# The last stage of a gradient kernel: a row-wise side for its products, left rows turned on TensorE, input rows in mid-column

## The chip, the cores and the metric

The kernel runs on one core of one Trainium2 chip. The metric is device time in microseconds (us) of one execution. The engines: TensorE (PE, matmuls; PEld loads its weights), VectorE (DVE), ScalarE (ACT), GpSimd (POOL) and SyncE (SP). SP, ACT and POOL also issue DMAs, each on a queue of its own and in the order of its program; the profile calls POOL's queue q0, SP's q1 and ACT's q10.

## The reference, cut to what matters

A layer normalisation feeds two branches whose outputs are added to the input: an attention with a recurrent memory (64 segments of 32 rows, 8 memory rows handed from segment to segment, 32 heads of 128) and a dense layer with squared relu. The kernel computes the output and all gradients for a given `grad_out`.

```python
for s in range(n_seg):
    h = jnp.concatenate([mem, xs], axis=1)          # 8 memory rows and 32 rows of the segment
    q, k, v = (jnp.einsum('btd,dhe->bhte', h, W) for W in (Wq, Wk, Wv))
    scores = jnp.where(mask, jnp.einsum('bhqe,bhke->bhqk', q, k) * scale, -1e9)
    o = jnp.einsum('bhqk,bhke->bhqe', softmax(scores), v)
    o = jnp.einsum('bhte,hed->btd', o, Wo)
    mem = o[:, :M, :]
    outs.append(o[:, M:, :])
...
return x + A(xn) + B(xn)
_out, _vjp = jax.vjp(f, A_x, A_mem0, A_Wq, A_Wk, A_Wv, A_Wo, B_w1, B_b1, B_w2, B_b2)
_grads = _vjp(grad_out)
```

What matters here are the gradients of the four attention weights. Each is one large product over all 2560 rows (2048 rows of segments and 64 times 8 memory rows): for Wq, Wk and Wv the normalised rows, transposed, times the gradient of q, k or v; for Wo the attention's rows, transposed, times the gradient of the output rows. The gradient of the input rows needs one more pass over 16 blocks of 128 rows.

## The kernel before, in words

The work is done in five stages: the dense branch, the forward chain over 64 segments, a preparation of the memory rows, the backward chain over the segments from last to first, and the last stage. Four segments make a block of 128 rows; there are NB = 16 blocks. Each block has also 32 "left" rows, the memory rows of its four segments.

**The backward chain** (lines 1088 to 1392). `B_ORDER` is a list, written out by hand, of the operations of one block's four steps, and `play` (line 581) walks it. A name with `L.` in front is an operation of a block's left rows; `+` and `-` shift it to the next or the one before. Each engine runs its instructions in this order. What the change touches:

- `gl` (line 1198) loads GT, a block's gradient rows with the feature axis on the partitions ([128, 4, 128]), on SP. The steps overwrite GT's memory rows by the gradients handed back (`HTf`).
- `gs` (line 1148) stores GT into the DRAM tensor S_GM on SP, in that same layout. The load of the GT after next waits for this store, since GT has two buffers.
- `vtr` (line 1245) is a DMA transpose of v on SP into b_vl; POOL copies it to b_vT (line 1252), and TensorE's scores and products follow.
- `so` (line 1151) stores the gradients of q, k and v into S_GB. `nt` and its store (lines 1184 to 1191) transpose a block's left rows gvL, gkL and gqL by DMA to gNat and store them into S_GL. For the last block (b = 0) both are issued by ACT instead of SP.
- `xt` (line 1177) reduces the left rows' input gradients to b_XL on VectorE (line 476), in one buffer, and `sl` (line 1181) stores it into S_XGL on SP.
- At the end the first memory's gradient is transposed by TensorE (line 1389), copied out of PSUM by VectorE to gm (line 1391) and stored. gm takes the memory of the buffer gON, which the last block's gNat of v uses as well.

**The last stage** (lines 1397 to 1508) goes over 16 "columns" (`COLS`: which weight, which quarter of its 4096 columns). A column's data is one tile gn of [128, 20, 1024] (16 blocks, then 4 tiles of left rows), in three buffers taken in turn: p5a lies over Wo and the chain's gv, p5b and p5c over the other weights. `rows_of` (line 1414) fills it: the Wo columns by plain loads of S_ON and S_OL, the others by 16 DMA transposes of S_GB on SP and plain loads of S_GL. Columns 0 and 1 are loaded on POOL's queue, later ones on SP's. Column i + 2 is loaded as column i starts.

The other side of the product is resident: GOc [128, 20, 512] for the Wo columns and HNc for the rest. `slot_side` (line 1406) fills each by four DMA transposes on SP (of S_GM, of S_HT) and four plain loads of left rows.

Per column TensorE makes eight products into eight PSUM banks, each a sum of 20 matmuls (line 1505): in column 0 the eight go side by side, block by block in `ORDER` (15 down to 0, then the left ones); in the others one product after the other. `leave` (line 1474) copies each out of PSUM on ScalarE and stores it on POOL's queue. Behind each column `input_rows` (line 1442) handles one block of input rows: five loads on POOL's queue (XT, XL, gb, xn, gi), a copy on VectorE (line 1448), four transposes on TensorE into ps_rows (line 1457), some arithmetic on VectorE, ScalarE and POOL, and a store. The loads at the stage's beginning are issued in the program's order (`manual_schedule`); the order of the rest is left to the scheduler.

Of the kernel before, what the change touches and what calls it, by code (L numbers as in the profile page):

```python
# [10 lines left out]
BF16 = mybir.dt.bfloat16  # L11
# [15 lines left out]
def kernel(  # L27
# [93 lines left out]
    S_GM = dram.tile([P, DC, S], BF16, name="S_GM")  # L121
# [815 lines left out]
    with sb("la", 2) as la, sb("ls", 2) as ls, sb("lo", 1) as lo_, sb("wg", 2) as wg, psum("lpp", 1) as lpp, psum("lr", 4) as lr:  # L937
# [168 lines left out]
    with sb("bq", 1) as bq, sb("bt", 1) as bt, sb("bs", 2) as bs, sb("be", 1) as be, psum("bpp", 1) as bpp, psum("br", 4) as br:  # L1106
# [17 lines left out]
        def block(b):  # L1124
            if b not in blk:
# [3 lines left out]
                          "XT": (bt, [P, DC, SPB, SEG], F32), "R4": (bt, [P, D], F32)}  # L1129
# [7 lines left out]
        def left(b):  # L1137
# [10 lines left out]
            o["gs"] = lambda: dma(S_GM[:, :, b * P:(b + 1) * P], gts[b][:])  # L1148
# [34 lines left out]
            for t, n in enumerate("qkv"):  # L1183
                def nt(n=n):

                    tag = "gNat" if b > 0 else {"k": "gNat", "v": "gON", "q": "gOT"}[n]
                    st[n] = bt.tile([P, KH, P], BF16, name="gNat", tag=tag)
                    (nc.sync if b > 0 else nc.scalar).dma_start_transpose(st[n][:], B_[src[n]][:].rearrange("p k g r -> p k (g r)"))
                o[n + "tr"] = nt
                o[n + "st"] = lambda n=n, t=t: (dma if b > 0 else nc.scalar.dma_start)(S_GL[b].rearrange("g r t c -> (g r) t c")[:, t, :],  # L1190
# [207 lines left out]
    with sb("p5a", 1) as p5a, sb("p5h", 1) as p5h, sb("p5", 2) as p5, sb("p5g", 1) as p5g, \  # L1398
            sb("p5b", 1, "right") as p5b, sb("p5c", 1, "right") as p5c, \
            tc.tile_pool(name="p5ps", bufs=8, space=bass.MemoryType.PSUM) as p5ps:  # L1400
# [5 lines left out]
        def slot_side(t_, srcT, src):  # L1406
            for dc in range(DC):
                nc.sync.dma_start_transpose(t_[:, 0:NB, dc * P:(dc + 1) * P], srcT[:, dc, :])
            lv = src.rearrange("(c q r) d -> c q r d", q=16, r=SEG)
            for c in range(NLC):  # L1410
                dma(t_[:, NB + c, :], lv[c][:, 0:M, :])
            return t_

        def rows_of(i, g, blocks, left_):

            t_ = (p5a, p5b, p5c)[i % 3].tile([P, RC_ALL, CW], BF16, name="gn5", tag="gn%d" % (i % 3))
            q = pdma if i < 2 else dma
            if blocks is None:
                for b in range(NB - 4, -1, -4):
                    q(t_[:, b:b + 4, :], S_ON[b:b + 4, g].rearrange("b p c -> p b c"))  # L1420
            else:
                for b in range(NB - 1, -1, -1):
                    nc.sync.dma_start_transpose(t_[:, b, :].rearrange("p (k e) -> p k e", k=KH),
                                                blocks(b)[:, g].rearrange("p k r -> p (k r)"))
            for j in range(SPB):
                q(t_[32 * j:32 * j + 32, NB:RC_ALL, :], left_(g).rearrange("(c j) r x -> j r c x", j=SPB)[j])
            return t_


        COLS = [(3, 0), (3, 1), (2, 0), (2, 1), (2, 2), (3, 2), (2, 3), (1, 0), (1, 1), (1, 2), (3, 3), (1, 3), (0, 0),  # L1430
                (0, 1), (0, 2), (0, 3)]
        got = {}

        def loads(i):
            if i < len(COLS):
                t, g = COLS[i]
                if t == 3:
                    got[i] = rows_of(i, g, None, lambda g: S_OL[:, g])
                else:
                    got[i] = rows_of(i, g, lambda b: S_GB[b, t], lambda g: S_GL[:, g, :, t, :])  # L1440

        def input_rows(b):

            XT = p5.tile([P, DC, P], F32, name="XT5", tag="XT5")
            pdma(XT[:], S_XG[b])
            XL = p5.tile([P, DC, SPB, M], F32, name="XL5", tag="XL5")
            pdma(XL[:], S_XGL[b])
# [96 lines left out]
```

## Time and profile before

| what | value |
|---|---|
| time of three runs (median) | 3051.87, 3058.38, 3061.96 us (3058.38) |
| the profiled execution, from first to last instruction | 3059.8 us; no other time of it is listed |
| PE, PEld, DVE, ACT, POOL busy | 88%, 45%, 43%, 33%, 22% |
| DMA | 566.78 MB, mean 185 GB/s; q1 58.8% of the 16 engines' span, q0 13.5%, q10 0.4% |
| mean granted clock of TensorE | 0.971 |
| matmuls of the last stage (line 1505) | 2560, 379 to 385 ns each in the mean, overlapping |
| copies out of PSUM in the last stage (line 1476) | 128, 586 ns |

How to read it: an instruction's row has its start and its length in us, its engine, line, operation and tiles (out<-in), and in brackets how long the engine sat idle before it and what ended that. "SPq" or "ACTq" is a queue's sequencer: the time there is the issue of a DMA, not its transfer. The chain of waits follows the work that ended last back through what released each step. A share of DMA of 1.00 means that all 16 engines are busy.

### The profile page before, as it was taken

How to read it: one execution, taken by the hardware profiler on the slowest of the kernel's cores; microseconds unless marked ns; L12 is line 12 of the kernel's file. 1: busy time of each engine (PE TensorE's matmuls, PEld its weight loads, DVE VectorE, ACT ScalarE, POOL GpSimd, SP SyncE). 2: the span in 40 equal slices, each digit the busy share in tenths (PEclk: the TensorE clock that was granted, in tenths of full speed). 3: DMA queues.
4: the chain of work that ended last, by engine and by line, in shares of the span. 5: the costliest groups of instructions: out<-in, count | busy, mean ns of one | idle time of the engine just before them, and what ended most of it. 6: DMA issues, size and time to landing. Idle time of an engine off the chain costs nothing. (4 is left out here: it accounts for less than half of the span.)

```text
span 3059.8 us, 109712 instructions
## 1 busy us (share of the span) xinstructions
PE 2705.4 (88%) x48600; PEld 1386.8 (45%) x48600; DVE 1319.5 (43%) x3581; ACT 994.7 (33%) x2306; POOL 658.0 (22%) x1264
## 2 busy tenths in 40 slices
PE   8997899999999886877799899998989559999998
PEld 4453444444444444446444444444444224444443
DVE  5452566666666664334345444544545201100010
ACT  2422444444444444323333333333333101111111
POOL 0000000000000000113343433434343213322222
PEclk9998999999999998999999999999999879999999
DMA  9548375766767767777577676776777899898991
GB/s 257 185 146 250 101 188 161 189 181 172 190 168 182 165 157 192 229 230 220 149 173 174 190 187 164 177 203 169 176 200 175 238 192 217 194 211 207 204 207 39
DMA packets 794559, 566.78 MB, mean 185 GB/s; under 512 B 579409, under 2 KB 681570, under 8 KB 790754
## 3 DMA queue, kind: packets, MB, share of 16 engines
q1 hardware_dynamic: 748322, 430.47, 58.8%
q0 software_dynamic: 40528, 126.53, 13.5%
q8 instruction: 381, 6.24, 0.9%
q10 hardware_dynamic: 5232, 2.75, 0.4%
q14 instruction: 96, 0.79, 0.1%
HBM read 193.61 MB, written 238.56 MB: 141 GB/s over the span
## 5 line engine op out<-in xcount | busy, mean ns | idle before, releaser
L1505 PE MATMUL ps_gw<-gn,HNc 128*128 128x512 bf16 x1920 | 416.4, 379 | 0.0
L1505 PEld LDWEIGHTS <-HNc 128*128 128x128 bf16 x1920 | 187.8, 98 | 223.9
L374 ACT CAST f_N<-ps_proj 128x512 bf16<-128x512 f32 x320 | 185.9, 581 | 243.9 <-PE ps_proj L392 223.4
L1476 ACT CAST wt<-ps_gw 128x512 bf16<-128x512 f32 x128 | 74.4, 586 | 503.5 <-PE ps_gw L1505 474.4
L392 PEld LDWEIGHTS <-X 128*32 128x32 bf16 x6144 | 153.3, 97 | 161.3 <-DVE X L482 13.9
L835 POOL COPY kM<-f_kT 128x256 bf16<-128x256 bf16 x64 | 25.6, 401 | 786.7 <-DVE f_kT L377 594.9
L1459 DVE TENSOR_TENSOR gx<-ps_rows,gb 128x512 f32<-128x512 f32 x16 | 11.1, 692 | 420.5 <-PE ps_rows L1457 418.2
L1505 PE MATMUL ps_gw<-GOc,gn 128*128 128x512 bf16 x640 | 142.2, 385 | 54.8 <-DMA GOc<-S_GM 54.8
L460 PE MATMUL ps_gR<-Wk,gk 128*32 128x512 bf16 x2048 | 146.7, 386 | 19.4 <-ACT gk L374 12.9
L392 PE MATMUL ps_proj<-Wk,X 128*32 128x512 bf16 x2048 | 135.4, 384 | 12.6 <-DVE X L482 6.9
L460 PE MATMUL ps_gR<-Wq,gq 128*32 128x512 bf16 x2048 | 141.6, 382 | 1.2 <-issue 1.2
L374 ACT CAST gk<-b_pp 128x256 bf16<-128x256 f32 x192 | 68.8, 377 | 208.3 <-PE b_pp L547 146.6
L1477 POOL DMA_DIRECT2D out_dram<-wt x128 | 69.2, 541 | 309.5 <-ACT wt L1476 309.4
L1239 POOL COPY PD<-b_P 32x320 bf16<-32x320 bf16 x256 | 114.9, 449 | 95.3 <-PE b_pp L1292 64.4
L460 PE MATMUL ps_gR<-Wv,gv 128*32 128x512 bf16 x2048 | 133.4, 379 | 0.3 <-issue 0.3
L392 PE MATMUL ps_proj<-Wo,GT 128*32 128x512 bf16 x2048 | 123.9, 384 | 7.9 <-POOL GT L1203 6.7
L392 PE MATMUL ps_proj<-Wq,X 128*32 128x512 bf16 x2048 | 128.7, 382 | 0.0
L460 PE MATMUL ps_R<-Wo,OT 128*32 128x512 bf16 x2048 | 126.4, 388 | 0.0
L469 PE MATMUL ps_sum<-identF,R 128*128 128x128 f32 x512 | 102.4, 295 | 24.6 <-ACT R L374 18.4
L392 PE MATMUL ps_proj<-Wv,X 128*32 128x512 bf16 x2048 | 124.1, 378 | 0.0
L1505 PEld LDWEIGHTS <-gn 128*128 128x128 bf16 x640 | 63.4, 99 | 132.3 <-issue 59.6
L374 ACT CAST gON<-ps_proj 128x512 bf16<-128x512 f32 x128 | 74.9, 585 | 143.2 <-PE ps_proj L392 141.5
(260 smaller groups left out, 5128.0 us busy)
## 6 DMA issues: line engine op xcount, KB each, us to landing
S_A<-f_N SPq DMA_DIRECT2D x64, 512.0 KB
out_dram<-wt POOLq DMA_DIRECT2D x142, 128.0 KB, 4.6
S_A<-f_N SPq DMA_DIRECT2D x64, 256.0 KB
S_GB<-gv SPq DMA_DIRECT2D x32, 512.0 KB
S_GB<-gq SPq DMA_DIRECT2D x32, 512.0 KB
S_GB<-gk SPq DMA_DIRECT2D x32, 512.0 KB
b_kN<-S_A POOLq DMA_DIRECT2D x63, 256.0 KB, 5.0
b_qN<-S_A POOLq DMA_DIRECT2D x63, 256.0 KB, 5.4
```

The costliest lines, as they stand in the source:

```text
L374: nc.scalar.copy(out, in_)
L392: nc.tensor.matmul(o, lhsT=hT[:, dc, :], rhs=x, start=(dc == 0), stop=(dc == DC - 1), tile_position=(0, 32 * g))
L460: nc.tensor.matmul(o, lhsT=XT(k, g), rhs=x, start=(first and k == 4 * h), stop=(last and k == 4 * h + 3), tile_position=(0, 32 * g))
L469: nc.tensor.transpose(st["T"][:, c * P:(c + 1) * P], R4()[:, c * P:(c + 1) * P], identF[:])
L835: o["km"] = lambda: nc.gpsimd.tensor_copy(B_["kM"][:, :, :, lc], T["kT"][:, :, :, 0:M])
L1239: nc.gpsimd.tensor_copy(PD[32 * g:32 * g + 32, g], C["P"][32 * g:32 * g + 32, :, 0:L])
L1459: nc.vector.tensor_tensor(out=gx[:], in0=ps[:], in1=gb[:], op=ALU.add)
L1476: nc.scalar.copy(wt[:], ps[:])
L1477: pdma(dst, wt[:])
L1505: nc.tensor.matmul(ps[:], lhsT=l(rc), rhs=r(rc), start=(n == 0), stop=(n == RC_ALL - 1))
```

## The change

- S_GM takes the gradient rows row-wise, [16, 128, 512]. In the chain `gs` turns GT by a DMA transpose on SP into a new tile GN (one buffer), and a new operation `gst` stores GN into S_GM. For the last block TensorE turns GT in four transposes, and ScalarE copies the result out.
- `nt` turns the last block's left rows on TensorE, in two halves of four transposes for each of v, k and q, copied out by ScalarE and VectorE; their stores go on SP's queue.
- GOc is split into six tiles (block 0, blocks 1 to 3, three times four blocks, the left rows) and loaded plainly on POOL's queue, between the quarters of column 0. `ORDER` is now 1 to 19, then 0.
- The tile of every third column (p5a) is split into five: four quarters of four blocks, and the left rows. Columns 0, 1 and 2 are loaded on POOL's queue; column (3, 2) is now the third.
- The input rows' loads become a function of their own, issued one block ahead. `input_rows` stays behind column 0 and then goes into the middle of each column, after four of its eight products. The whole stage is in the program's order.
- The last column's results are stored on SP's queue.

```diff
-    S_GM = dram.tile([P, DC, S], BF16, name="S_GM")
+    S_GM = dram.tile([NB, P, D], BF16, name="S_GM")
...
-        "d31 vc d41 tu1 qeb0 kp1 qp1 keb1 qg0 qea1 L.gl+ kea1 kg1 qeb1 qg1 rb ra tb ta L.H3 kla1 HT",
+        "d31 vc d41 tu1 qeb0 kp1 qp1 keb1 qg0 qea1 L.gl+ L.gst kea1 kg1 qeb1 qg1 rb ra tb ta L.H3 kla1 HT",
...
-            o["gs"] = lambda: dma(S_GM[:, :, b * P:(b + 1) * P], gts[b][:])
+            def gs():
+                if b > 0:
+                    nc.sync.dma_start_transpose(B_["GN"][:], gts[b][:].rearrange("p c r -> p (c r)"))
+                else:
+                    ps["gm"] = tr("ps_gm")
+                    for c in range(DC):
+                        transpose_to(ps["gm"][:, c * P:(c + 1) * P], gts[b][:, c, :])
+                    acp(B_["GN"][:], ps["gm"][:].rearrange("p (c d) -> p c d", c=DC))
+            o["gs"] = gs
+            o["gst"] = lambda: dma(S_GM[b], B_["GN"][:].rearrange("p c d -> p (c d)"))
...
-                    (nc.sync if b > 0 else nc.scalar).dma_start_transpose(st[n][:], B_[src[n]][:].rearrange("p k g r -> p k (g r)"))
+                    if b > 0:
+                        nc.sync.dma_start_transpose(st[n][:], B_[src[n]][:].rearrange("p k g r -> p k (g r)"))
+                    else:
+                        for p in range(2):
+                            pt = tr("ps_tr")
+                            for k in range(4):
+                                transpose_to(pt[:, k * P:(k + 1) * P],
+                                             B_[src[n]][:, 4 * p + k].rearrange("p g r -> p (g r)"))
+                            (acp, vcp)[p](st[n][:, HALF[p], :], pt[:].rearrange("p (k e) -> p k e", k=4))
...
-        ORDER = list(range(NB - 1, -1, -1)) + list(range(RC_ALL - 1, NB - 1, -1))
+        ORDER = list(range(1, RC_ALL)) + [0]
...
+        def columns(i):
+            if i % 3 == 0:
+                return [p5a.tile([P, 4, CW], BF16, name="gn5", tag="gn%d" % q) for q in range(RC_ALL // 4)]
+            t_ = (p5b, p5c)[i % 3 - 1].tile([P, RC_ALL, CW], BF16, name="gn5", tag="gn5")
+            return [t_[:, 4 * q:4 * q + 4] for q in range(RC_ALL // 4)]
...
+        def loads(i):
+            if i < len(COLS):
+                got[i] = columns(i)
+                eng = pdma if i < 3 else dma
+                for q in range(NB // 4):
+                    load_quarter(i, q, eng)
+                load_left(i, eng)
...
+        def go_rows(n):
+            if n < 5:
+                r = (slice(0, 1), slice(1, 4), slice(4, 8), slice(8, 12), slice(12, 16))[n]
+                pdma(GO[n][:], S_GM[r].rearrange("b p d -> p b d"))
+            else:
+                lv = gflat.rearrange("(c q r) d -> c q r d", q=16, r=SEG)
+                for c in range(NLC):
+                    pdma(GO[n][:, c, :], lv[c][:, 0:M, :])
...
-            loads(0)
-            slot_side(GOc, S_GM, gflat)
-            loads(1)
-            slot_side(side, S_HT, S_XN[:])
+        got[0] = columns(0)
+        load_quarter(0, 0, pdma)
+        load_quarter(0, 1, pdma)
+        for n in range(1, 6):
+            go_rows(n)
+            if n < 3:
+                load_quarter(0, 1 + n, pdma)
+        load_left(0, pdma)
+        go_rows(0)
+        loads(1)
+        loads(2)
+        input_loads(NB - 1)
+        for dc in range(DC):
+            nc.sync.dma_start_transpose(side[:, 0:NB, dc * P:(dc + 1) * P], S_HT[:, dc, :])
...
-            for js in ([jobs] if i == 0 else [[x] for x in jobs]):
+            last = i == len(COLS) - 1
+            for x, js in enumerate([jobs] if i == 0 else [[x] for x in jobs]):
+                if x == 4:
+                    input_rows(NB - 1 - i)
+                    if not last:
+                        input_loads(NB - 2 - i)
...
-                    leave(ps, dst)
-            input_rows(NB - 1 - i)
+                    leave(ps, dst, dma if last else pdma)
+            if i == 0:
+                input_rows(NB - 1)
+                input_loads(NB - 2)
```

More of the change, by code (lines that the diff above doesn't have):

```diff
@@ L1442, in input_rows @@
         def input_rows(b):
[L1444 to L1447, printed above, removed]
+            XT, XL, gb, xn, gi = (rows[b][n] for n in ("XT", "XL", "gb", "xn", "gi"))
             nc.vector.tensor_copy(XT[:].rearrange("p c (j r) -> p c j r", j=SPB)[:, :, :, 0:M], XL[:])
-            gb = p5.tile([P, D], F32, name="gb5", tag="gb5")
-            pdma(gb[:], S_GXNB[b * P:(b + 1) * P, :])
```

80 lines of the change are left out of this document (40 added, 40 removed).

## The prediction

> **What bounds the kernel now.** I read the chain of waits first, its longest pieces from the end of the backward chain to the second column of the last stage. Each row has its start, its length (us) and what it was.
>
> ```profile
> 2409.55 20.80 DMA gNat<-b_gkL
> 2431.05 16.92 DMA gNat<-b_gvL
> 2451.05 4.79 DMA GOc<-S_GM
> 2456.00 3.06 DMA gNat<-b_gqL
> 2459.07 2.40 SPq L1408
> 2462.04 2.73 SPq L1408
> 2464.82 4.76 DMA GOc<-S_GM
> 2469.82 35.03 PE ps_gw L1505 x153
> 2505.41 2.56 ACT wt L1476 x5
> 2509.05 4.27 issue
> 2515.23 4.98 DMA XL<-S_XGL
> 2521.80 36.06 PE ps_gw L1505 x160
> ```
>
> Behind 2409.5 us the chain computes nothing: three DMA transposes of the last block's left rows and four of GOc follow one another, and the first column starts at 2469.82. A second hole lies between the first column (35.0 us, to 2504.85) and the second (2521.80): 16.9 us, ending on the loads of the first input rows. From there TensorE is full until 3047.46. The third hole is the input rows behind the last column:
>
> ```profile
> 3012.47 0.44 PE ps_rows L1457 x4
> 3012.91 34.55 PE ps_gw L1505 x160
> ...
> 3053.68 2.85 issue
> 3056.53 0.60 POOLq L1539
> ```
>
> From 3047.46 to the end at 3059.8 are 12.3 us. From the first transpose on, the three holes hold 60 + 17 + 12 = 89 us of a span of 3059.8. That span is the profiled execution's time here; the median of the three runs, 3058.38, is 1.4 less, and I carry that over.
>
> **Part 1, the backward chain.** Each block's store of the gradient side becomes a transpose (SBUF to SBUF, 128x512) plus a plain store on SP. The tightest of the 14 blocks with a following load on SP:
>
> ```profile
> 1787.91 0.58 SPq L1148 DMA_DIRECT2D S_GM<-GT  x1
> 1788.53 0.63 SPq L1181 DMA_DIRECT2D S_XGL<-b_XL  x1
> 1791.54 0.58 SPq L1201 DMA_DIRECT2D GT<-S_GT  x1
> 1792.17 0.62 SPq L1190 DMA_DIRECT2D S_GL<-gNat  x1
> 1796.33 1.30 SPq L1247 DMA_TRANSPOSE b_vl<-S_A  x1
> ```
>
> The trace has no 128x512 transpose; the row nearest to its issue is b_vl's 1.30 us, for twice the size, so at most 0.7 us more than the store, and the new store costs some 0.6: 1.3 us of SP. The reload of GT must now wait for the transpose instead of for the store (3.6 us from issue). Queued behind are S_GL's store and b_vl, for whose vT POOL and then TensorE wait. SP idles 3.5 us before b_vl here (4 to 5 elsewhere), so 1.3 us is hidden. gNat's transpose of gqL, twice as large, landed in 3.06 us on idle DMA engines; in the chain the engines are loaded to 0.61 of their time, and saturated only behind it (columns: stretch, us, busy PE, PEld, DVE, ACT and POOL, clock, DMA share, GB/s):
>
> ```profile
> 2360.00:2400.00 40.00, 36.53 (x957) 18.84 (x952) 20.43 (x56) 14.42 (x41) 14.38 (x28) 1.00 0.61 131
> 2400.00:2440.00 40.00, 13.62 (x280) 7.70 (x279) 7.34 (x22) 2.92 (x9) 10.40 (x16) 0.74 1.04 343
> ```
>
> I take 0, between no cost and 1 us per block (15 us). A gain is excluded: nothing that the chain waits for leaves it.
>
> **Part 2, the last left rows on TensorE.** 24 transposes for k, v, q and 4 for the gradient side, with seven copies out of PSUM on ScalarE and VectorE.
>
> ```profile
> 2203.98 0.40 PE L165 MATMUL ps_tr<-ident,gON 128*128 128x128 bf16 x4
> 2414.44 0.60 PE L1389 MATMUL ps_m<-identF,gm 128*8 128x128 f32 x4
> ```
>
> 28 at 0.1 us are 2.8 us; the copies, 0.6 us each on two engines, add about 2.4 where the four PSUM buffers run round. TensorE's tail then ends near 2420 instead of 2415.0. This is off the path if part 3 is right.
>
> **Part 3, what opens the first column.** Two things must be there: the first quarter with GOc's blocks 1 to 3, and a free PSUM bank for each of the eight products. The last bank is freed by the copy gm on VectorE. gm writes into memory from which S_GL's rows of v are stored, and it is queued behind the reduction b_XL, which waits until block 1's S_XGL has been stored. Both waits stand in the trace, hidden today:
>
> ```profile
> 2412.01 3.38 SPq L1181 DMA_DIRECT2D S_XGL<-b_XL  x1
> 2434.94 0.88 DVE L476 TENSOR_REDUCE b_XL<-ps_sum 128x32 f32<-128x128 f32 x4 [21.05 <-DMA S_XGL<-b_XL]
> 2447.99 0.34 ACTq L1190 DMA_DIRECT2D S_GL<-gNat  x1
> 2451.45 0.68 DVE L1391 CAST gm<-ps_m 8x512 bf16<-8x512 f32 x1 [15.62 <-DMA S_GL<-gNat]
> ```
>
> So these small stores are late next. A 64 KB store took over 20 us, because POOL's column loads ran beside it. From 2411 to 2423 the queues moved:
>
> ```profile
> DMA packets 2447, 4.57 MB, mean 381 GB/s; under 512 B 772, under 2 KB 1493, under 8 KB 2446
> ## 3 DMA queue, kind: packets, MB, share of 16 engines
> q0 software_dynamic: 883, 3.38, 75.1%
> q1 hardware_dynamic: 881, 1.00, 23.7%
> ```
>
> POOL's queue (q0) and SP's (q1) advance packet for packet, and q0's packets are over three times as large. POOL will start earlier than today:
>
> ```profile
> 2394.92 1.08 PE ps_proj L392 x20
> ```
>
> ```profile
> 2404.37 2.99 POOL L1420 DMA_DIRECT2D gn<-S_ON  x4 [13.93 <-DMA S_GB<-gv]
> ```
>
> Column 0 is one tile of 40 KB per partition today, over Wo and gv, and waits until gv is stored at 2404.4. In quarters, the four block tiles lie over Wo alone, free after the last ps_proj at 2396.0, and only the left rows wait for gv. From 2396.5 POOL issues 7.7 MB (4.2 of column 0, 2.0 of GOc, 0.5 and 1.05 of left rows). Then comes GOc's block 0, which waits for S_GM's last store, and POOL stands still there. Meanwhile SP must move 4.65 MB (S_GB 3.15, the rest in small pieces) until that store and S_GL's v are through. Together 12.4 MB at the 381 GB/s above take 32.5 us: 2429. From S_GL's issue at 2447.99 to gm are 3.5 us today, of which 0.7 are its 262 KB at that rate; 2.8 to land brings gm to 2431.8, and with its 0.7 us the first matmul starts at **2432.5**, 37.3 us earlier. Bounds: 2422 (the queues done as TensorE's tail ends) and 2452 (first rival).
>
> **Part 4, the first column and its input rows.** 35.0 us as before: the quarters are in by 2429, and the left rows are read only 26 us after the start. It ends at 2467.5. POOL's next loads are columns 1 and 2 (10.5 MB) and only then XT and XL. POOL's rate from 2429 to 2441:
>
> ```profile
> q0 software_dynamic: 1046, 4.02, 90.8%
> ```
>
> 4.02 MB in 12 us is 0.335 MB per us: 10.6 MB from 2431 end at 2462.6, XT and XL (0.3 MB) and their landing add 3 to 4: 2466, level with the column's end. I take a wait of 2 us, between 0 and today's 16.9; with the first copy out of PSUM (0.6) and ps_rows (0.44) column 1 starts at **2470.5** instead of 2521.8: 51.3 us.
>
> **Part 5, the other columns.** The second input rows are wanted after four products (17.3 us) of column 1. Their loads are issued behind the first ones' arithmetic on POOL:
>
> ```profile
> 2528.54 1.15 POOL L1471 TENSOR_TENSOR gi<-gx,gi 128x512 bf16<-128x512 f32 x1 [0.68 <-DVE gx L1469]
> ```
>
> From ps_rows (2520.72) to the end of gi are 9 us, 1.6 for three issues, 5.0 for landing (XL above), up to 3 for stores queued ahead: 16 to 19 against 17.3. I take 2. Later rows have a whole column of 35 us for the same 16: nothing. Columns 1 to 15 keep their 525.7 us, plus 0.4 for one more ps_rows inside. Their loads have room:
>
> ```profile
> SPq L1423 <- PE ps_rows L1457: 96.0, 10, 26.9
> ```
>
> SP waited 96 us, ten times, for TensorE to free a column's buffer.
>
> **Part 6, the end.** What is left after the last product is the copy (0.6), an SP issue (0.6) and a landing, below POOL's median:
>
> ```profile
> out_dram<-wt POOLq DMA_DIRECT2D x142, 128.0 KB, 4.6
> ```
>
> The chain's end has 3.3 us from the last issue on, so 4.5 and the hops between them: about 5.0 us (4.2 to 6.5) instead of 12.3: 7.3 us.
>
> **Sum:** 51.3 - 2 - 0.4 + 7.3 = 56.2 us. 3059.8 - 56.2 = 3003.6 of span; 1.4 less for the median: **3002 us**.
>
> **Rivals.** (a) The small stores starve. If POOL's large packets run beside SP's all the time, SP keeps 1.00 MB per 12 us: the 3.6 MB behind gv's stores take 43 us from 2405, 2448, and the first column starts at 2452. That is 19.5 us later, less the 2 of part 4 (XT is there by then): 3020. For it: the 21 us above. Against it: POOL stops at GOc's block 0 until SP has caught up. [...]
>
> (b) The second hole moves rather than goes. If columns 1 and 2 come slower than 0.335 MB per us (HNc's four transposes run beside them), XT is late again; with today's 16.9 us column 1 starts 13.9 us later: 3016. For it: XT is queued behind 10.5 MB. Against it: small packets beside large ones cost q0 little.
>
> (c) The change doesn't do what it says: both (a) and (b), the first column waiting for the very stores and bytes that the transposes waited for: 3002 + 19.5 + 14 = 3035.
>
> (d) Slower: the transposes stretch the chain. Place: SP between GT's reload and b_vl, 14 times. Under full load the transpose of gkL took 20.80 us against 3.06 for gqL on idle engines; midway, at 11.9, GT's reload comes 8.3 us late, 9.5 with the further store, 6 beyond SP's idle time: 84 us, 3086. It decides from 4.0 us of delay per block beyond the 3.5 of idle time. Against it: DMA engines at 0.61, not 1.04, in the chain.
>
> **Chances.** Forecast (2991 to 3012) 0.56, (a) 0.17, (b) 0.15, (c) 0.05, (d) 0.05, near nothing gained 0.02. The range reaches from 2988 (first column at 2422, no wait for XT or the second rows) to 3027 (a, or b with part of part 1's bound) and leaves out (c), (d) and small ends. 0.3% (9 us) is about what a measurement here tells from no change: faster by more 0.93, within 0.02, slower 0.05.
>
> **What will show it.** No DMA transpose between the chain's end and the first ps_gw; VectorE's gm waiting for S_GL near 2432 as the last releaser of the first ps_gw; ps_rows right behind column 0; SP idle before b_vl at 2 us or more in each block; the last ps_gw about 5 us before the end. Wrong if the backward chain ends later than 2415, if the first column starts after 2440, or if column 1 waits over 5 us for XT.

## The result and the profile after

The changed kernel takes 3014.02 us (median of 4, 3005.99 to 3024.51) against 3058.96 of the kernel before on the same chip (median of 4): a ratio of 0.9859, 95% interval 0.9832 to 0.9885. The forecast was 3002 with a range of 2988 to 3027. Of the 56.2 us forecast, the profiled execution shows 48.7 (span 3011.1 us, 3013.04 with what lies around it), so 7.5 us of the forecast are missing there. The medians differ by 44.9 us, 11.3 less than forecast.

The chain of waits of the changed kernel shows where the three holes have gone (start, length in us, what it was):

```profile
2404.88 17.26 DMA GOc<-in_grad_out_dram
2422.14 11.04 issue
2433.18 0.59 PE ps_gw L1554
...
2468.91 2.55 ACT wt L1493 x5
2471.46 0.46 issue
2471.92 11.09 DMA out_dram<-wt
...
2490.70 5.87 DMA XL<-S_XGL
...
2496.99 1.09 PE ps_rows L1474 x4
```

The first column starts at 2433.18 instead of 2469.82. Its results leave from 2468.91 on, and then the chain goes through one of its stores, which took 11.09 us to land, and through the load of XL to the second input rows at 2496.99. The "issue" of 11.04 us is no cause, only a place where this view loses the thread. The timeline of the same kernel has the releasers (start, length, engine, line, operation, tiles, count, and in brackets the idle time before and what ended it):

```profile
2416.60 6.21 SPq L1208 DMA_DIRECT2D S_GL<-gNat  x1
2422.86 1.21 SPq L1191 DMA_DIRECT2D S_XGL<-b_XL  x1
2424.16 0.41 SPq L1158 DMA_DIRECT2D S_GM<-b_GN  x1
2431.37 0.88 DVE L476 TENSOR_REDUCE b_XL<-ps_sum 128x32 f32<-128x128 f32 x4 [13.93 <-DMA S_XGL<-b_XL]
2432.18 0.56 POOL L1508 DMA_DIRECT2D GOc<-S_GM  x1 [9.91 <-DMA S_GM<-b_GN]
2434.88 49.40 SPq L1528 DMA_TRANSPOSE HNc<-S_HT  x4
2473.66 0.23 DVE L1471 COPY XT<-XL 128x128 f32<-128x128 f32 x1 [40.58 <-DMA XL<-S_XGL]
2473.99 0.63 PE L1474 MATMUL ps_rows<-identF,XT 128*128 128x128 f32 x4 [3.72 <-DVE XT L1471]
```

Three things are to be seen. SP needs 6.21 us for the issue of one store, and so block 1's S_XGL, ordered behind it, goes out only at 2422.86 and has landed at 2431.3. b_XL on VectorE waits 13.93 us for that store, and behind b_XL stands gm, which frees the last PSUM bank. And HNc's four transposes, 9.33 us of SP in the kernel before, take 49.40 us, beside GpSimd's loads of columns 1 and 2, while XT and XL wait in GpSimd's queue. Column 1 starts at 2474.45, 47.1 us earlier than before. The second rows then cost TensorE 5.11 us more, and from the last product (3007.37) to the end are 3.8 us.

### The profile page after: what moved, and what is told of

Its sections match the earlier page's. It is cut to its first block, busy times and chain, and to the rows that moved or that the text cites. A ratio compares the mean times of both kernels' runs of the same rounds, so it can differ in the third digit from the quotient of the medians.

```text
span 3011.1 us, 109612 instructions
## 1 busy us (share of the span) xinstructions
PE 2701.5 (90%) x48480; PEld 1389.0 (46%) x48628; DVE 1321.8 (44%) x3584; ACT 997.8 (33%) x2310; POOL 666.2 (22%) x1273
## 5 line engine op out<-in xcount | busy, mean ns | idle before, releaser
L835 POOL COPY kM<-f_kT 128x256 bf16<-128x256 bf16 x64 | 25.8, 403 | 782.7 <-DVE f_kT L377 590.9
L460 PE MATMUL ps_gR<-Wk,gk 128*32 128x512 bf16 x2048 | 149.4, 391 | 19.6 <-ACT gk L374 12.4
L469 PE MATMUL ps_sum<-identF,R 128*128 128x128 f32 x512 | 102.8, 295 | 24.7 <-ACT R L374 18.4
L1270 POOL COPY b_vT<-b_vl 128x1024 bf16<-128x1024 bf16 x64 | 66.5, 1039 | 185.1 <-PE ps_sc L437 154.8
```

The costliest lines, as they stand in the source:

```text
L460: nc.tensor.matmul(o, lhsT=XT(k, g), rhs=x, start=(first and k == 4 * h), stop=(last and k == 4 * h + 3), tile_position=(0, 32 * g))
L469: nc.tensor.transpose(st["T"][:, c * P:(c + 1) * P], R4()[:, c * P:(c + 1) * P], identF[:])
L835: o["km"] = lambda: nc.gpsimd.tensor_copy(B_["kM"][:, :, :, lc], T["kT"][:, :, :, 0:M])
L1270: nc.gpsimd.tensor_copy(vT[:, :, :, 0:SEG], C["vl"][:])
```

## How the runs are compared

The last ps_proj of the backward chain ends anywhere from 2392.0 to 2420.3 us in the profiles below, a scatter of 28 us. Of it, 19 us are there before the backward chain's first load of GT (1438.1 to 1457.2 us), where the kernels are still alike; behind that load they differ only in how S_GM is stored, which the account of part 1 below takes up. So I measure the **stretch** from the end of that projection to the end of the span, read off the timelines, and set the ratio of the timed runs beside it. All times in us:

| kernel | last projection ends | first column | column 1 | last product ends | span | stretch | ratio to before, 95% |
|---|---|---|---|---|---|---|---|
| before | 2396.0 | 2469.8 | 2521.6 | 3047.4 | 3059.8 | 663.8 | 1 |
| changed | 2393.8 | 2433.2 | 2474.5 | 3007.4 | 3011.1 | 617.4 | 0.9859 (0.9832 to 0.9885) |
| changed, again | 2393.9 | 2433.1 | 2481.7 | 3008.5 | 3012.3 | 618.4 | 0.9862 (0.9844 to 0.9879) |
| a: left rows by DMA | 2411.5 | 2455.0 | 2493.9 | 3024.5 | 3028.0 | 616.5 | 0.9837 (0.9807 to 0.9867) |
| b: side by DMA | 2409.5 | 2484.3 | 2521.2 | 3046.7 | 3050.3 | 640.9 | 0.9925 (0.9898 to 0.9953) |
| c: rows behind | 2399.2 | 2438.5 | 2479.4 | 3003.7 | 3016.1 | 616.8 | 0.9856 (0.9832 to 0.9881) |
| d: gate | 2407.9 | 2432.5 | 2495.1 | 3025.4 | 3029.2 | 621.3 | 0.9885 (0.9855 to 0.9914) |
| d2: gate, other tiles | 2420.3 | 2446.1 | 2505.3 | 3033.8 | 3037.5 | 617.3 | 0.9893 (0.9863 to 0.9924) |
| e: rows early | 2407.2 | 2446.5 | 2483.9 | 3032.2 | 3036.0 | 628.8 | 0.9884 (0.9855 to 0.9914) |
| f: both | 2400.2 | 2424.8 | 2478.3 | 3020.6 | 3024.3 | 624.2 | 0.9873 (0.985 to 0.9895) |
| g: loads held | 2418.3 | 2450.8 | 2546.3 | 3072.1 | 3075.9 | 657.6 | 0.9985 (0.9964 to 1.0006) |
| k: column 2 on SP | 2392.0 | 2433.7 | 2470.2 | 2999.9 | 3003.7 | 611.6 | 0.984 (0.9814 to 0.9867) |
| j: all three | 2405.4 | 2430.2 | 2472.4 | 3004.9 | 3008.6 | 603.3 | 0.9809 (0.979 to 0.9827) |
| m: all, stores on ScalarE | 2401.5 | 2435.7 | 2473.6 | 2998.3 | 3002.1 | 600.6 | 0.9794 (0.977 to 0.9818) |

In the stretch the change is worth 663.8 - 617.4 = 46.4 us, 1.5% of the span, within the interval of the ratio (1.2% to 1.7%). The two profiles of the changed kernel agree within 1.0 us.

## The experiments

My theory from the profile after: the side's plain loads and the rows' new place gave the gain; the first column is now opened by block 1's S_XGL store; and what is missing are two waits for input rows, late because GpSimd's queue (POOL in the views) holds 10 MB ahead of them. The rivals: the left rows' turning opened the column; the loads' bytes are the limit.

**a. The last left rows by DMA again.**

```diff
-                    else:
-                        for p in range(2):
-                            pt = tr("ps_tr")
...
+                    (nc.sync if b > 0 else nc.scalar).dma_start_transpose(st[n][:], B_[src[n]][:].rearrange("p k g r -> p k (g r)"))
...
+                o[n + "st"] = lambda n=n, t=t: (dma if b > 0 else nc.scalar.dma_start)(S_GL[b].rearrange("g r t c -> (g r) t c")[:, t, :],
```

> The changed kernel, with one part undone: the last block's left rows are turned by DMA transposes issued by ScalarE again, and ScalarE issues their stores. Theory (the turning on TensorE opens the first column): gm's tile is the one that the left rows of v used, so gm waits for their store, which in the kernel before came only at 2451.5 us behind starved transposes. The first column should open near 2452 instead of 2433.2, column 1 near 2488 instead of 2474.5, and 12 to 17 us of that should reach the end: about 3029 us (3022 to 3040). Rival (the first column is opened by block 1's S_XGL store and b_XL, at 2431.4, whatever the left rows do): first column near 2433, total 3014 within 3 us.

The stretch is 616.5 us, no more than the changed kernel's. The column opens 43.6 us behind the last projection instead of 39.4, and column 1 only 1.7 later. From the timeline of this kernel:

```profile
2449.92 0.89 DVE L476 TENSOR_REDUCE b_XL<-ps_sum 128x32 f32<-128x128 f32 x4 [17.94 <-DMA S_XGL<-b_XL]
2451.89 0.33 ACTq L1200 DMA_DIRECT2D S_GL<-gNat  x1
2453.16 0.56 POOL L1500 DMA_DIRECT2D GOc<-S_GM  x1 [13.64 <-DMA S_GM<-b_GN]
2454.26 0.68 DVE L1401 CAST gm<-ps_m 8x512 bf16<-8x512 f32 x1 [3.45 <-DMA S_GL<-gNat]
```

S_GL's v lands within 2.4 us of its issue, because GpSimd stands still for S_GM just then and no large load is under way (from 2445 to 2454 its queue moves 0.11 MB). gm is thus free 3.45 us behind b_XL, not the 19 that I had expected. So the theory fell in its size: turning the left rows on TensorE moves the opening by 4 us, which the wait for XT takes back. That part of the change is worth nothing measurable.

**b. The side by DMA transposes again.**

```diff
+    S_GM = dram.tile([P, DC, S], BF16, name="S_GM")
...
+            o["gs"] = lambda: dma(S_GM[:, :, b * P:(b + 1) * P], gts[b][:])
...
+        for dc in range(DC):
+            nc.sync.dma_start_transpose(GOc[:, 0:NB, dc * P:(dc + 1) * P], S_GM[:, dc, :])
```

> The changed kernel, with one part undone: the gradient side is stored column-wise again and brought in by four DMA transposes and four loads on SyncE, all else as changed. Theory (the transposed side is what held the first column in the kernel before, where it ended last): SyncE issues the transposes behind its stores, from about 2433, and they crawl beside GpSimd's loads as the input side's do in the changed kernel (49.4 us for four): the first column opens between 2455 and 2490, column 1 35 us later, and the total is 3034 to 3060 us. Rival (what counted was only that the column's own loads left early, in quarters): first column within 5 us of 2433, total 3014 to 3020 us.

The chain of waits:

```profile
2437.90 25.54 DMA S_GM<-GT
2463.48 0.04 issue
2463.52 6.81 SPq L1501
...
2477.30 6.83 DMA GOc<-S_GM
2484.12 0.20 issue
2484.32 36.56 PE ps_gw L1535 x160
```

The last S_GM store took 25.54 us beside GpSimd's loads, and only then could the transposes start. The first column opens 74.9 us behind the last projection, where the kernel before had 73.8, and the stretch is 23.5 us longer than the changed kernel's. The time is the theory's; its mechanism is so only in part. The four transposes did not crawl: they took SP 17.1 us (6.81 for the first, 10.28 for the other three), far from the 49.4 expected. What came late was the store ahead of them. The 23.0 us which b still gains on the kernel before are the wait for XT (14.4 us before, none here) and the 8.7 us at the end. No run undoes the earlier loads of the input rows or the split of column 0 into quarters, so that the 14.4 us come from the former is read from the order of the loads and not shown.

**c. The input rows behind each column.**

```diff
-                if x == 4:
-                    input_rows(NB - 1 - i)
-                    if not last:
-                        input_loads(NB - 2 - i)
...
-            if i == 0:
-                input_rows(NB - 1)
-                input_loads(NB - 2)
+            input_rows(NB - 1 - i)
+            if not last:
+                input_loads(NB - 2 - i)
```

> The changed kernel, with one part undone: each column's input rows behind its last result and not in mid-column, and the last column's stores from GpSimd; the rows' loads are still issued a column ahead. Theory (the prediction's last term): what follows the last column's matmuls is 12 us as in the kernel before instead of 3.7, that is +8.3 us; the second rows have a whole column for their load, so the 5.1 us that TensorE waits for them in the changed kernel go: together +3 us, 3017 us. Rival (the place in the column is worth nothing, since TensorE has work either way): what follows the last column stays under 6 us, and only the 5.1 us go: 3009 us.

The end costs 12.4 us (3003.7 to 3016.1), 8.6 more. But columns 1 to 15 take 524.3 us (2479.4 to 3003.7) instead of 532.9: 8.6 less, and the stretch is the same (616.8), where the theory asked for 3 us more and the rival for 5 less. So the mid-column place does bring what was forecast for it, and gives it back at once, since the second rows are then wanted half a column earlier than their loads come. Their price is 8.0 us and not the 5.1 of the wait: the step from the second rows to the third is 37.91 us in the changed kernel and 34.97 in every later column. The stages table of the changed kernel (columns: stretch, us, busy PE, PEld, DVE, ACT and POOL, clock, DMA share, GB/s) shows why:

```profile
2474.00:2497.00 23.00, 17.84 (x84) 8.19 (x85) 3.59 (x6) 3.61 (x8) 10.25 (x17) 0.98 1.14 206
2497.80:2502.60 4.80, 4.58 (x13) 1.71 (x13) 2.89 (x5) 0.41 (x2) 1.15 (x1) 0.50 1.05 246
2502.60:2530.00 27.40, 27.29 (x126) 12.40 (x127) 0.70 (x2) 3.52 (x6) 7.66 (x13) 0.99 1.15 211
```

In the 4.8 us shown behind the wait the granted clock is 0.50; by the same view it is 0.50 from 2497.0 to 2502.9, and half of these 5.9 us are the 2.9 us lost beyond the wait itself. Not every wait was followed by a low clock: behind one of 3.1 us in k the clock was 0.53 for 3.6 us, behind one of 10.6 us in the second profile of the changed kernel 0.51 for 4.4 us, but behind the one of 3.7 us before column 1 in the changed kernel it was 1.00 (2474.5 to 2479). So 3.1 us were enough in k and 3.7 were not in the changed kernel; what decides it, no run shows.

**d and d2. No store ahead of the first column.** b_XL of the last block and gm get tiles that wait for no store. In d these are tiles in whose memory GOc is loaded; in d2 other ones.

```diff
-                st["XL"] = bt.tile([P, DC, SPB, M], F32, name="b_XL", tag="XL")
+                st["XL"] = bt.tile([P, DC, SPB, M], F32, name="b_XL", tag="XL" if b > 0 else "gST0")
...
-            gm = bt.tile([M, D], BF16, name="gm", tag="gON")
+            gm = bt.tile([M, D], BF16, name="gm", tag="gqL")
```

> The changed kernel, with the last b_XL and gm in tiles of their own, so that neither waits for a store. Theory (the first column is opened by these two waits and not by its data): TensorE's first column starts at about 2419.5, right behind the last matmul of the chain at 2418.3, and ends near 2455; but the input rows' XT still lands near 2473, so column 1 starts no earlier than 2472 and the total stays 3014 within 3 us: the 14 us move into a wait for XT. Rival (the first column is bound by 12.4 MB at 381 GB/s): it starts after 2427, or starts and stops for its loads, and ends near 2466; total again unchanged.

> As the run before it with the last b_XL and gm in tiles whose last readers are TensorE's (a turned block of the last segment, the left rows of q), instead of two that GpSimd's side loads overlie: no wait for a store before the first column, and none added for GpSimd. Theory: TensorE's first column starts 24 to 26 us behind GpSimd's first load of the stage (39.1 in the changed kernel) and ends near 59, but the rows' XT comes near 79 to 85 as before, so column 1 starts there and the total is 0 to 6 us above the changed kernel's (ratio to the kernel before 0.986 to 0.988). Rival (the 12.4 MB of the first column bound it): the first column starts at 25 but is stopped for loads and ends past 68.

In d (tags qNL and gOL, both in the pool be) the column starts 24.6 us behind the last projection, 1.2 behind TensorE's last matmul of the chain, and runs without a stop:

```profile
2432.48 34.69 PE L1554 MATMUL ps_gw<-GOc,gn 128*128 128x512 bf16 x160 [1.17 <-issue]
2439.55 0.75 POOL L1508 DMA_DIRECT2D GOc<-S_GM  x1 [26.12 <-DMA S_GL<-gNat]
2494.20 1.08 PE L1474 MATMUL ps_rows<-identF,XT 128*128 128x128 f32 x4 [27.02 <-DVE XT L1471]
```

So the gate is shown: 14.8 us of the changed kernel's opening are the two waits for stores. The bytes did not hold the column even though GpSimd stood 26.12 us for GOc's memory, a wait that my choice of tiles had made. All of it came back as a wait for XT. d2 has no such wait on GpSimd, opens 25.8 us behind the last projection, and waits 23.68 us for XT; its stretch is the changed kernel's to 0.1 us. Its timed ratio lies 0.003 above, at the edge of the two intervals; with one profile that stays open.

**e and f. The first two blocks' rows loaded ahead of column 2,** alone and with d2's tiles.

```diff
         loads(1)
-        loads(2)
         input_loads(NB - 1)
+        input_loads(NB - 2)
+        loads(2)
...
             if i == 0:
                 input_rows(NB - 1)
-                input_loads(NB - 2)
```

> The changed kernel with the loads of the first two blocks' input rows issued ahead of column 2's loads instead of behind them and behind column 0's results. Theory (both waits for XT are queueing behind 5 MB on GpSimd's queue): the wait of 3.7 us before column 1 and that of 5.1 us for the second rows go, column 2's loads still come in time, and the total is 8 to 9 us less: ratio to the kernel before 0.983, or 3005 us. Rival (the rows are late because the queue is full, wherever they stand in it, and column 1 or 2 then waits for its own loads instead): total within 3 us of the changed kernel, ratio 0.985 to 0.987.

> Both of these together: b_XL and gm wait for no store, and the first two blocks' input rows are loaded ahead of column 2. Theory: the first column starts at 24 to 26 us behind GpSimd's first load, ends near 59, column 1 starts at 60 instead of 80.4, the second rows do not wait: 25 to 29 us less than the changed kernel, ratio to the kernel before 0.976 to 0.978, or about 2987 us. Rival (the loads then bound it: GpSimd's queue has 18 MB ahead of column 1's end, and it stands for the last store of the side): column 1 or the rows wait 10 to 15 us more, gain 10 to 17 us, ratio 0.980 to 0.983.

Both theories missed. e is 11.4 us slower than the changed kernel. Its first rows come earlier (76.3 us behind the last projection instead of 80.2), and then TensorE stands 21.6 us for the second:

```profile
2507.59 0.56 POOL L1494 DMA_DIRECT2D out_dram<-wt  x1 [20.63 <-DMA gn<-S_ON]
...
2520.46 0.69 DVE L1481 TENSOR_REDUCE m<-gb 128x1 f32<-128x512 f32 x1 [34.92 <-POOL gb L1477]
...
2522.66 0.22 DVE L1471 COPY XT<-XL 128x128 f32<-128x128 f32 x1
```

In the traces of e and of the changed kernel GpSimd issues a load or a store only when an earlier one of its own, eight back, has landed. In the changed kernel the load of XT at 2457.81 waits 2.43 us for column 2's first quarter, issued at 2440.14 with seven others between; in e column 0's first store (2486.39) waits 3.75 us for that quarter and the second (2507.59) 20.63 us for the next, each eight issues back. With the ten loads of rows ahead of them, column 2's 5 MB are issued from 65.3 us behind the last projection on (46.4 in the changed kernel), right ahead of column 0's stores. These stores wait for them to land (20.63 us), and GpSimd's product gb stands behind the stores; VectorE waits 34.92 us for gb, and the copy of the second XT, loaded since 2479.2, waits behind it in VectorE's order. f opens the first column at 24.7 us as the gate theory has it, and then waits 17.84 us for XT and 13.25 for the second rows. XL was issued only once the second of column 1's quarters had landed, and took 20.8 us to land. The loads ran beside HNc's transposes (56.23 us for the four), which an earlier gm had also let start 2.4 us earlier; how much of the wait that made is not shown:

```profile
2438.87 56.23 SPq L1529 DMA_TRANSPOSE HNc<-S_HT  x4
...
2455.99 0.55 POOL L1466 DMA_DIRECT2D XL<-S_XGL  x1 [10.16 <-DMA gn<-S_ON]
```

**g. GpSimd's loads held until the chain is done.**

```diff
+        go_rows(0)
         load_quarter(0, 0, pdma)
...
         load_left(0, pdma)
-        go_rows(0)
```

> The changed kernel with the load of the side's last block, which waits for the chain's last S_GM store, put at the head of GpSimd's loads, so that no load of this stage runs beside the end of the chain. Theory (the loads starve SyncE's stores and slow TensorE's fetches there): the hole of 2.3 us in TensorE's last segment goes, the chain ends 2 to 3 us earlier against its own last projection, a SyncE issue takes under 1.5 us each instead of up to 6.2, the first column opens 6 to 9 us behind the chain's end instead of 14.9; but every load starts 20 us or more later, XT comes near the same time or up to 8 us later, and the total is 0 to 8 us more than the changed kernel: ratio 0.986 to 0.989. Rival (the stores are slow by themselves, whatever GpSimd loads): the issues stay slow, the first column opens 15 us or more behind the chain's end, total 10 us or more above the changed kernel.

The near half came as expected. The chain's last matmul ends 21.0 us behind the last projection instead of 24.6, the hole of 2.30 us in TensorE's last segment is gone, and SP's issues are short:

```profile
2434.86 0.33 SPq L1208 DMA_DIRECT2D S_GL<-gNat  x1
2435.24 0.42 SPq L1191 DMA_DIRECT2D S_XGL<-b_XL  x1
2437.40 0.32 SPq L1158 DMA_DIRECT2D S_GM<-b_GN  x1
2438.86 0.88 DVE L476 TENSOR_REDUCE b_XL<-ps_sum 128x32 f32<-128x128 f32 x4 [0.49 <-PE ps_sum L469]
2442.86 87.06 SPq L1528 DMA_TRANSPOSE HNc<-S_HT  x4
2450.76 0.59 PE L1554 MATMUL ps_gw<-GOc,gn 128*128 128x512 bf16 x1 [11.50 <-DMA GOc<-S_GM]
```

S_GL's issue takes 0.33 us where it took 6.21, and b_XL no longer waits. So SP's slow issues and 3.6 us of the chain are the price of GpSimd's early loads. The far half was mis-sized by far: the stretch is 657.6 us, not 617 to 625. All 12.4 MB and both next columns now run beside HNc (87.06 us for four transposes), column 0 stops 11.7 us for its left rows, and XT comes 46.9 us later. The early start of the loads is worth 40 us, far more than what it costs the stores.

**The changed kernel again, and k and j.** k puts column 2's loads on SP's queue, ahead of HNc. j adds d2's tiles, the early rows, and column 1's loads ahead of the side's last block.

```diff
-                eng = pdma if i < 3 else dma
+                eng = pdma if i < 2 else dma
```

```diff
-        go_rows(0)
         loads(1)
-        loads(2)
+        go_rows(0)
         input_loads(NB - 1)
+        input_loads(NB - 2)
+        loads(2)
```

> The changed kernel as it is, beside the two that follow and under their conditions. Every theory: from the last projection of the chain to the end 616 to 619 us (617.4 in the profile of the changed kernel), and a ratio to the kernel before of 0.983 to 0.989. If that stretch comes out otherwise, the stretches compared so far are not comparable.

> The changed kernel with column 2's five loads of 5 MB on SyncE's queue, ahead of the four transposed loads of HNc, instead of on GpSimd's ahead of the rows' loads. Theory (the rows come late because GpSimd, which also stores and computes, stands in order behind 5 MB of loads that it issues only as earlier ones land, and because HNc's transposes take turns with those): XT is there before column 0 ends, column 1 starts 76 to 77 us behind the last projection of the chain instead of 80.7, the second rows do not wait and TensorE does not fall to half pace behind them: from that projection to the end 605 to 609 us instead of 617.4. Rival (the bytes are the limit, whoever issues them): XT as late as before, 615 to 620 us, or column 3 waits for HNc and it is more.

> The same, and with it: the last b_XL and gm in tiles that wait for no store, column 1's loads ahead of the side's last block, and the first two blocks' rows right behind these. Theory (gate, queue and shared engines are the three things that cost the changed kernel time there, and each alone only moves the wait to the next): the first column starts 25 us behind the last projection, column 1 at 59 to 62, the rows do not wait: 586 to 594 us from that projection to the end, ratio to the kernel before 0.976 to 0.979. Rival (one of them still binds: XT is not there at 58, or HNc, now later, holds column 3): 600 us or more.

The changed kernel again: here the first rows waited 10.59 us and the second not at all, with nearly the same stretch. The two waits are one lateness that shows at one place or the other: 3.72 + 5.11 us of waits in one profile and 10.59 in the other, 11.8 and 12.7 us with what the low clock behind them cost. In k, XT is copied 72.9 us behind the last projection (79.9 and 86.6 in the two profiles of the changed kernel), 3.7 us ahead of the first copy out of PSUM; column 1 starts 78.2 behind it, where 76 to 77 were expected, since the first column opened 2.3 us later. The second rows still wait 3.08 us. 5.8 us come of it, less than the 8 to 12 expected, and the rival (the bytes) is out for the first rows: the same bytes, issued elsewhere, were in time. HNc's transposes also start 8.4 us later in k than in the changed kernel (49.5 against 41.1 behind the projection), so k does not tell GpSimd's order from HNc's place as the cause. In j the first column opens at 24.8, column 1 starts at 67.0, and the stretch is 603.3, 14.1 less than the changed kernel's but short of the 594 expected. The timeline names one reason:

```profile
2462.27 0.56 POOL L1508 DMA_DIRECT2D GOc<-S_GM  x1 [21.65 <-DMA S_GM<-b_GN]
2467.49 3.57 PE L1555 MATMUL ps_gw<-GOc,gn 128*128 128x512 bf16 x8 [4.59 <-DMA GOc<-S_GM]
```

The last block's store, now between more loads, came so late that the column stood 4.59 us for its last chunk. The second rows stood 4.71 us, behind column 0's last two copies and stores.

**m. The last block's stores on ScalarE's queue, and the first rows' arithmetic ahead of column 0's last two results,** with all of j.

```diff
-            o["gst"] = lambda: dma(S_GM[b], B_["GN"][:].rearrange("p c d -> p (c d)"))
+            o["gst"] = lambda: (dma if b > 0 else nc.scalar.dma_start)(S_GM[b], B_["GN"][:].rearrange("p c d -> p (c d)"))
...
+                o[n + "st"] = lambda n=n, t=t: (dma if b > 0 else nc.scalar.dma_start)(S_GL[b].rearrange("g r t c -> (g r) t c")[:, t, :],
...
+                    if i == 0 and n == 6:
+                        input_rows(NB - 1)
```

> The run before it, in which TensorE stood 4.6 us for the side's last block (its store lay on SyncE's queue behind loads and slow stores until 57 us behind the last projection) and 4.7 us for the second rows (VectorE's copy of XT stood behind the first rows' sums, and these behind GpSimd's product, queued behind column 0's last two stores). Here the last block's stores of side and left rows go out on ScalarE's own queue, and the first rows' arithmetic stands ahead of column 0's last two results. Theory (what is slow is the crowded queue, not the store: a store issued by ScalarE in the kernel before landed in 3.5 us beside the same loads): the first column runs without a hole from 25 to 58 us behind the last projection, column 1 starts at 59 to 62, the rows do not wait: 587 to 593 us to the end, ratio to the kernel before 0.976 to 0.978. Rival (the engines that move the data are full, whichever queue asks): the store lands as late as before, and the stretch stays above 600 us.

```profile
2426.84 0.33 ACTq L1158 DMA_DIRECT2D S_GM<-b_GN  x1
2434.70 0.33 ACTq L1208 DMA_DIRECT2D S_GL<-gNat  x1
2435.07 0.58 ACT L374 COPY gNat<-ps_tr 128x512 bf16<-128x512 bf16 x1 [10.91 <-DMA S_GM<-b_GN]
2435.70 37.62 PE L1555 MATMUL ps_gw<-GOc,gn 128*128 128x512 bf16 x160 [9.67 <-ACT gNat L374]
```

The number, 600.6 us, is just the rival's (above 600) and not the theory's (587 to 593), but not for the rival's reason: the store of the side no longer holds anything (its load is issued at 2439.10), column 0 has no hole, and neither rows wait. The theory's ground was misread, though. The 3.5 us of the store in the kernel before were not beside the same loads, for GpSimd's queue moved nothing from 2448 to 2451.5. Here the store landed 8.0 us after its issue, no sooner than from SP in the changed kernel (7.5); in j, issued by SP behind one of column 2's loads, it took 23.8. But ScalarE's next issue of S_GL came only at 2434.70. An S_GB store that SP had issued at 2407.69 landed at 2434.6, just ahead of it; that the issue waited for this store is read from the order in time and not tested. Behind the issue stood ScalarE's copy of the last left rows, which frees the PSUM bank, and the column opened 34.3 us behind the last projection instead of 24.8. m has the lowest ratio of the study: 0.9794 (0.977 to 0.9818) against 0.9859 for the changed kernel, 17 us of stretch. Its interval overlaps that of j (0.979 to 0.9827). The 9.5 us of its opening remain; they were not tried further.

## Why the prediction was right, step by step

- **Part 1, nothing in the chain: right as far as it can be told.** SP idles 2.0 to 4.7 us before b_vl in the 14 blocks of the changed kernel (3.5 to 5.5 before), so the 1.3 us are covered there; in other row-wise profiles single blocks go down to 0.15 (d) and 0.10 us (f). From the first load of GT in the backward chain to the last projection are 951.2 us before and 952.3 in b, which both store column-wise, and 949.7 to 965.8 (mean 956.8) in the 12 profiles that store row-wise, 955.1 in the changed kernel's. The lowest leave no price at all; 0.4 us per block, the difference of the means over 14, can't be told from the scatter. Rival (d), 9.5 us per block, is out.
- **Part 2, TensorE's tail to 2420: right** (2418.3, and 3.6 us of that are GpSimd's loads, by g). But a shows that this part of the change, turned back, costs nothing.
- **Part 3, the first column at 2432.5: near in time (2433.2), wrong in its last releaser.** Part of the nearness is luck: in this profile the last projection ended 2.2 us earlier than in the profile before (2393.8, 2396.0), and from it the column opened after 39.4 us where 36.5 were forecast. gm waits for no store of its own; it stands behind b_XL and block 1's S_XGL store. Both were named, but the sign to look for named only S_GL. What S_XGL waited for was SP's slow issues (6.21 us for S_GL's ahead of it), on which the prediction put no price. Rival (a) did not come: GpSimd stood 9.91 us for the last S_GM store, as the argument against it had it; that this stand is what held it off is not tested by itself.
- **Part 4, XT 2 us late: mis-sized.** Column 1 started 3.95 us after the forecast 2470.5. The forecast had XT and XL land 3 to 4 us behind column 2's bytes. The term that failed is the rate of 0.335 MB per us. From 2433 to 2469, with HNc's transposes under way, GpSimd's queue moved 3.85, 3.10 and 3.54 MB in 12 us each, 0.29 MB per us in the mean: that was rival (b)'s condition, and 10.6 MB take 36.4 us at it instead of 31.6. XL was issued at 2460.33 and its data were there 13 us later, behind loads not yet landed and beside HNc. Its own sign said wrong if column 1 waits over 5 us: 3.72 in one profile, 10.59 in the other, of the 16.9 that rival (b) had. What spoke against (b), that small packets cost GpSimd's queue little, fits the kernel before from 2429 to 2441, where that queue moved 4.02 MB beside 1061 packets of SP's and ScalarE's queues (0.52 MB). It is not borne out here: the 3.85, 3.10 and 3.54 MB went beside 691, 857 and 957 packets of SP's queue (0.21, 0.22 and 0.24 MB). No run tests whether HNc's packets are the reason.
- **Part 5, 2 us for the second rows: mis-sized.** 5.11 us of wait and 2.9 of half clock. The step that failed is "16 to 19 us against 17.3": from the first ps_rows (2473.99) to XL's landing (2490.70 + 5.87) were 22.6 us, because GpSimd's product stood behind column 0's last two stores, and these behind copies that waited for the first stores' memory (11.09 us to land). Columns 1 to 15 without it, 532.9 - 5.1 - 2.9 = 524.9, are 1.2 under the forecast 526.1.
- **Part 6, 5.0 us at the end: 3.8.** c has 12.4 with the old order.

The 7.5 us are thus 3.95 for column 1, 4.8 for columns 1 to 15 (532.9 against 528.1 with the 2 us), less 1.2 at the end. By the mark of the last projection, without the 2.2 us of luck, the forecast stretch was 607.6 us, and 9.8 are missing: 2.9 in the opening of the first column, 2.1 in that column, 1.2 in the step to column 1, 4.8 in columns 1 to 15, less 1.2 at the end. The 2.1 are a misread term: the 35.0 us taken for column 0 are the chain's row of 153 of its 160 matmuls, while the timeline has 36.5 before and 37.1 after. The largest part is one lateness of the rows' loads, which was sized twice at 2 us and came to 11.8 with the low clock behind it.

The median of 3014 lies in the stated range, but outside the 2991 to 3012 that were given a chance of 0.56. It is nearest to rival (b)'s 3016, which had 0.15, and (b)'s cause, rows late behind column loads slower than 0.335 MB per us, is what came. So the mechanism was right in the main (the first hole shrinks by the side's plain loads, as b shows), and the lateness of the rows in it was taken too small.

## What to carry to other kernels

GpSimd loads, computes and stores here in one order, so moving one load forward moved the wait to the next thing behind it: with the rows' loads ahead of column 2's (e), a store waited 20.63 us and VectorE 34.92 us for a product behind the stores. Ask what stands behind a load before moving it. Undoing each part by itself shows which part of a change pays: here the plain loads of the side (23.5 us), while the left rows' turning paid nothing and the rows' new place was given back until their loads were early enough. Compare from a mark close to the change when the rest of the program scatters more than the effect.

## What was not expected of the hardware

- The issue of a store on SP took 6.21 us beside GpSimd's loads and 0.33 us without them (g), while an issue from ScalarE took 0.33 us beside the same loads (m). In m itself SP's issue of S_XGL at 2425.30 took 6.82 us and ScalarE's of S_GM at 2426.84 took 0.33: what was slow there was the issue on SP's queue.
- The same four transposes of HNc took SP 9.33 us in the kernel before and 10.60 us in b, with GpSimd's loads done. Beside GpSimd's loads of columns 1 and 2 they took 42.8 to 87.1 us, and 25.2 to 37.4 in k, j and m, where column 2's loads stood ahead of them on SP's queue.
- Behind waits of 3.1 us (k), 5.1 us (changed kernel) and 10.6 us (its second profile) TensorE's granted clock was 0.53, 0.50 and 0.51 for 3.6, 5.9 and 4.4 us, which cost up to 2.9 us more; behind one of 3.7 us it was 1.00.
- In all twelve profiles with GpSimd's early loads, TensorE stops for 0.6 to 2.8 us in the middle of a group of matmuls of the last segment (2.30 in the changed kernel, to 2403.07), with no wait that the profile shows. Each time the stop ends 2.2 to 2.5 us behind the start of a 16 KB packet on queue q8, which the profile lists as "instruction". That packet comes 5.1 to 7.4 us behind the last projection there, against 3.6 in the kernel before and 2.6 in g, which have no such stop. So the instructions of TensorE seem to come late beside these loads; this is read from the order in time and not tested by itself.
